# Rounding theta's number of turns by the integer result of one multiplication

## The chip, the cores and the metric

The kernel runs on one core of a Trainium2 chip. It is measured in device microseconds of one execution. A profiled execution also leaves a trace, in which each instruction has its engine, its start and its duration, and in which releases between engines can be followed. The engines are called as the profile calls them where rows are meant (PE, DVE, ACT, POOL, SP) and by name in the text: TensorE, VectorE, ScalarE, GpSimd, and SyncE, which issues the transfers.

## The reference, cut to what matters

An attention over 4 batches, 12 heads, 448 tokens with mixing across heads is followed by a gated block, and that by a block which turns every feature by an angle. The change lies in this last block:

```python
def _moe2_ref(x, w_theta, w_tok_r, w_tok_i, w_ch):
    theta = x @ w_theta                              # (4, 448, 768) @ (768, 768)
    cos_t, sin_t = (np.cos(theta), np.sin(theta))
    zr = x * cos_t
    zi = x * sin_t
    yr = np.einsum('ts,bsd->btd', w_tok_r, zr)
    yi = np.einsum('ts,bsd->btd', w_tok_i, zi)
    u = x + (yr + yi)
    return (u + np.maximum(u @ w_ch, 0.0)).astype(np.float32)
```

Theta reaches several turns, and the sine of ScalarE is fed with angles between -pi and pi, so the kernel takes whole turns off theta first.

## The kernel before

The program is written engine by engine in a fixed order: a list of units, each with functions to run before and after it (`d.unit`, `d.pre`, `d.post`), is walked once, and every engine executes its own instructions in the order in which they were written. Nothing reorders them later.

The last block, `moe2`, is the part of the program from about 614 us on. The tokens of a batch come in chunks of 128; batches are taken in pairs, so that the last 64 tokens of two batches make one common chunk (c = 3): 14 chunks of two halves of 384 features, 28 halves in all. The units stand in this order: theta for the four chunks of batch 0 and the first chunk of batch 1; `tok` for batch 0 (six units, the product with w_tok); theta for the other two chunks of batch 1; `ch` for batch 0 (six units, the product with w_ch); `tok` for batch 1; theta for batch 2, and so on to `ch` for batch 3.

A theta unit is 18 matmuls (six slices of the contraction, three products of high and low parts of x and w_theta, L555). After the first half come six transposes of x into PSUM (L1053). PSUM has eight buffers of this kind, and TensorE waits when the next isn't released.

- `angles` (L1059 to L1073), one call for each half, runs behind the half's theta unit. On VectorE: n = theta / 2pi plus a large constant (L1064), the constant off again (L1065), which leaves the nearest whole number; r = theta - n C1 (L1067) and r - n C2 (L1068), where C1 + C2 = 2pi; then r is held between -pi and pi (L1069). On ScalarE: the absolute value of r, its sine as cosine, and the sine of r (L1070 to L1072). L1064 and L1067 read theta from PSUM; the others read SBUF.
- `rotate` (L1075 to L1094) is called one unit later, so VectorE has the angles of a half ahead of the rotation of the half before. VectorE multiplies x (in PSUM) by cosine and sine (L1091, or four half-height instructions L1087 for the common chunk), ScalarE rounds the products to the high part (`d.cast`, L548), and GpSimd takes the rest as the low part of z (`d.rest`, L551).
- `split_x2` (L1023) does the same for x itself, two chunks ahead: two casts on ScalarE, and two operations "x2s" on GpSimd (L551), for every second half. The theta of that chunk needs them.
- For the chunk of batch 1 among the first five, `rotate` is put off until the six `tok` units, so its PSUM buffers stay taken until then. Beside these `tok` units VectorE also adds the residual (L1114), splits u (L551) and turns four blocks of w_ch from 64-bit into two 32-bit numbers (L983 to L996, L988 with an operand of type uint32).

In a steady row of theta units VectorE repeats, for every half: L1091 twice (the half before), L1064, L1065, L1067, L1068, L1069. This is called a turn below. Between two turns of a chunk GpSimd runs two operations of z, and in every second turn the two of x2 as well.

Of the kernel before, what the change touches and what calls it, by code (L numbers as in the profile page):

```python
# [9 lines left out]
I32 = mybir.dt.int32  # L10
U32 = mybir.dt.uint32
AF = mybir.ActivationFunctionType
ALU = mybir.AluOpType
# [467 lines left out]
TO = ((1, 1, 1, 1, 1, 1), (1, 0, 1, 0, 1, 0), (1, 0, 1, 0, 1, 1), (0, 1, 1, 1, 1, 0))  # L481
KC = 4
KE = 3
MAGIC = 12582912.0
INV2PI = 1.0 / (2.0 * math.pi)
C1 = 6.28125
C2 = 2.0 * math.pi - C1
# [454 lines left out]
def moe2(d, left, win_es, last_u, m1_left):  # L942
    tc, nc, io = d.tc, d.nc, d.io
# [115 lines left out]
    def angles(b, c, half):  # L1059

        th = st.pop((b, c, half))
        tp = d.pools["t2"]
        n = tp.tile([128, 384], F32, tag="n", name="n")
        nc.vector.tensor_scalar(out=n, in0=th, scalar1=INV2PI, scalar2=MAGIC, op0=ALU.mult, op1=ALU.add)  # L1064
        nc.vector.tensor_scalar(out=n, in0=n, scalar1=MAGIC, scalar2=None, op0=ALU.subtract)  # L1065
        r = tp.tile([128, 384], F32, tag="r", name="r")
        nc.vector.scalar_tensor_tensor(out=r, in0=n, scalar=-C1, in1=th, op0=ALU.mult, op1=ALU.add)  # L1067
        nc.vector.scalar_tensor_tensor(out=r, in0=n, scalar=-C2, in1=r, op0=ALU.mult, op1=ALU.add)  # L1068
        nc.vector.tensor_scalar(out=r, in0=r, scalar1=PI_F, scalar2=-PI_F, op0=ALU.min, op1=ALU.max)  # L1069
        nc.scalar.activation(out=n, in_=r, func=AF.Abs)  # L1070
        nc.scalar.activation(out=n, in_=n, func=AF.Sin, scale=-1.0, bias=d.const["hpi"])
        nc.scalar.activation(out=r, in_=r, func=AF.Sin)  # L1072
        st[b, c, half] = ((n, r), st[b, c, "x"][half])  # L1073
# [119 lines left out]
    for b, c, i0 in chunks:  # L1193
        for half in range(2):
            d.post(i0 + half, angles, b, c, half)
# [104 lines left out]
```

## Time and profile before

| | us |
|---|---|
| three runs | 913.23, 915.72, 919.0 |
| median | 915.72 |
| profiled execution | 918.77 |
| its span, first to last instruction | 917.0 |
| VectorE busy in it | 679.8 |
| TensorE busy in it | 857.6 |

The span is 1.8 us shorter than the profiled execution's own time, which also holds what lies around the program. Starts in the rows are counted from the span's start. The granted clock is a share of TensorE's full speed: 1.00 is 2.4 GHz, 0.50 is 1.2 GHz. A row "x2" merges two instructions of one kind that follow each other. A bracket behind a row is the idle time of the engine just before it and what ended it; matmul ends are modelled, and spans on GpSimd are rough.

### The profile page before, as it was taken

To read this page: it belongs to the slowest core of one execution; us is meant where nothing else is said; L and a number is where in the kernel's file an instruction comes from. 1 tells how busy PE (TensorE), PEld (TensorE's weight loads), DVE (VectorE), ACT (ScalarE), POOL (GpSimd) and SP (SyncE) were. 2 spreads that over 40 slices of the span, in tenths; PEclk is the share of its full clock that TensorE was granted. 3 is DMA by queue.
4 is the path that set the end of the run, shared out by engine and by line. 5 is a ranking of instruction groups with operands and counts; after the bars stand their busy time and mean duration, and the time that the engine had idled before them with its cause. 6 is when DMAs were issued, how large, how long until landed. Compare 5 with 4: busy or idle time off the path is not lost.

```text
span 917.0 us, 29432 instructions
## 1 busy us (share of the span) xinstructions
PE 857.6 (94%) x12008; PEld 675.2 (74%) x12008; DVE 679.8 (74%) x1509; ACT 525.3 (57%) x1188; POOL 252.1 (27%) x453
## 2 busy tenths in 40 slices
PE   8789899999989999697899999999998999999998
PEld 2345556555656566486797988889897999999997
DVE  3787888788878887389989899859878349539421
ACT  5688789878988896365554655425535025315110
POOL 0163255225322632000000000015606316604511
PEclk9999999999999999899999999989998999999999
DMA  6557656765676545773376685896620302210301
GB/s 205 179 192 224 197 179 219 223 204 179 218 222 214 174 158 138 260 233 108 119 246 213 190 256 172 267 339 213 231 89 19 121 18 53 71 50 18 93 29 61
DMA packets 116343, 151.15 MB, mean 165 GB/s; under 512 B 26224, under 2 KB 100208, under 8 KB 116208
## 3 DMA queue, kind: packets, MB, share of 16 engines
q1 hardware_dynamic: 116208, 149.26, 51.3%
q8 instruction: 95, 1.56, 0.7%
q14 instruction: 40, 0.33, 0.1%
HBM read 78.38 MB, written 32.31 MB: 121 GB/s over the span
## 4 chain that ended last, share of the span: by engine, by line
PE 54%; DVE 22%; DMA 9%; ACT 5%; issue 5%; POOL 3%; SPq 1%; ACTq 0%; DVEq 0%; POOLq 0%
PE ps L555 30%; PE psC L302 7%; PE psB L244 6%; PE psA L219 5%; PE psD L354 5%; DMA blk<-s 2%; DVE da L611 2%; ACT e L258 2%; POOL vl L197 1%; DMA win<-win_d 1%; DVE dp L605 1%; ACT s L225 1%; DMA x2T<-xres 1%; DVE da L592 1%; DMA xraw<-xT 1%
## 5 line engine op out<-in xcount | busy, mean ns | idle before, releaser
L258 ACT ACTIVATE e<-psB,nmx 128x448 f32<-128x448 f32 x180 | 112.7, 634 | 33.8 <-DVE nmx L250 32.0
L331 DVE SCALAR_TENSOR_TENSOR al<-psC,ah 128x480 f16<-128x480 f32 x180 | 116.3, 647 | 16.0 <-ACT ah L325 15.1
L250 DVE TENSOR_REDUCE nmx<-psB 128x1 f32<-128x448 f32 x180 | 103.9, 618 | 18.8 <-PE psB L244 17.2
L302 PE MATMUL psC<-wr,e 64*64 64x60 f32 x5632 | 106.9, 221 | 10.9 <-issue 8.9
L302 PEld LDWEIGHTS psC<-wr,e 64*64 64x64 f32 x5632 | 93.5, 135 | 23.4 <-issue 11.5
L551 POOL TENSOR_TENSOR x2s<-x,x2s 128x384 fp32r<-128x384 f32 x28 | 29.6, 1082 | 288.1 <-DMA wth<-wth_d 213.4
L555 PE MATMUL ps<-wtok,z 128*128 128x448 f32 x504 | 104.8, 368 | 0.4 <-POOL z L551 0.4
L219 PE MATMUL psA<-k,q 64*64 64x448 f32 (+2 forms) x768 | 95.2, 549 | 9.1 <-ACT s L225 5.5
L244 PE MATMUL psB<-blk,kpre 64*64 64x448 f32 x720 | 102.0, 548 | 1.6 <-DMA blk<-s 0.8
L325 ACT ACTIVATE ah<-psC 128x480 f16<-128x480 f32 x180 | 93.2, 576 | 16.5 <-PE psC L302 16.2
L555 PEld LDWEIGHTS ps<-wtok,z 128*128 128x128 f32 x504 | 94.4, 188 | 10.0 <-POOL z L551 0.8
L354 PEld LDWEIGHTS <-vh 128*64 128x64 f16 x1536 | 56.6, 111 | 57.2 <-issue 52.8
L555 PE MATMUL ps<-wth,x2s 128*128 128x384 f32 x504 | 94.3, 343 | 2.1 <-DVE r L1067 1.1
L555 PEld LDWEIGHTS ps<-wth,x2s 128*128 128x128 f32 x504 | 89.3, 192 | 3.0 <-DVE r L1067 1.5
L225 ACT ACTIVATE s<-psA 124x896 f32<-124x896 f32 (+1 forms) x90 | 83.7, 930 | 13.0 <-PE psA L219 5.4
L555 PE MATMUL ps<-u,wch 128*128 128x448 f32 x432 | 89.9, 368 | 0.0
L555 PEld LDWEIGHTS ps<-u,wch 128*128 128x128 f32 x432 | 81.1, 188 | 8.1
L551 POOL TENSOR_TENSOR z<-zz,z 128x384 fp32r<-128x384 f32 x56 | 61.9, 1126 | 71.4 <-ACT z L548 71.3
L555 PE MATMUL ps<-win,x 128*128 128x512 f32 x252 | 63.3, 405 | 10.7 <-DVE x L551 6.4
L264 POOL TENSOR_SCALAR rc<-sum 128x2 f32<-128x2 f32 (+1 forms) x92 | 22.5, 244 | 179.1 <-ACT e L258 178.0
L280 POOL TENSOR_SCALAR wr<-w,rc 128x60 f32<-128x60 f32 x180 | 54.2, 315 | 57.7 <-DVE rc L269 39.4
L244 PEld LDWEIGHTS psB<-blk,kpre 64*64 64x64 f32 x720 | 36.7, 133 | 44.0 <-issue 24.2
(129 smaller groups left out, 1577.5 us busy)
## 6 DMA issues: line engine op xcount, KB each, us to landing
blk<-s SPq DMA_DIRECT2D x176, 210.0 KB
draw<-in_w_in SPq DMA_DIRECT2D x24, 256.0 KB
k<-in_kvT SPq DMA_DIRECT2D x24, 224.0 KB
xraw<-xT SPq DMA_DIRECT2D x24, 224.0 KB
xres<-xT SPq DMA_DIRECT2D x24, 224.0 KB
x2T<-xres SPq DMA_DIRECT2D x24, 224.0 KB
xres<-x2T SPq DMA_DIRECT2D x24, 224.0 KB
out<-uu SPq DMA_DIRECT2D x24, 224.0 KB
```

Of the source, the lines that this page charges most:

```text
L219: nc.tensor.matmul(ps[e][r, :S], q[p, o + r.start:o + r.stop], k[p], start=True, stop=True)
L225: nc.scalar.activation(out=out, in_=pair[:m, :, :S], func=AF.Copy, scale=0.125)
L244: nc.tensor.matmul(ps[e][c:c + 64, :S], kpre[k, e], blk[k], start=True, stop=True)
L250: nc.vector.tensor_reduce(out=nmx[r][:, e:e + 1], in_=ps[:, :S], axis=AX.X, op=ALU.max, negate=True)
L258: nc.scalar.activation(out=x, in_=ps[:, :S], func=AF.Exp, bias=m[:, e:e + 1], accum_out=sm[:, e:e + 1])
L280: nc.gpsimd.tensor_scalar(out=w, in0=wts[n], scalar1=rc[:, e:e + 1], scalar2=0.0, op0=ALU.mult, op1=ALU.add)
L302: nc.tensor.matmul(pc[r][h][c:c + 64, jc, :, SQ * e:SQ * e + SQ], x[p, c:c + 64], wr[r][e][p], start=(e == 0 and jc == 0), stop=(e == 1 an ...
L325: nc.scalar.activation(out=at_view(r, e, at[b, t][0]), in_=at_src(r, e), func=AF.Copy, scale=2.0 ** -17)
L331: nc.vector.scalar_tensor_tensor(out=al, in0=at_src(r, e), scalar=2.0 ** -17, in1=ah, op0=ALU.mult, op1=ALU.subtract)
L354: nc.tensor.matmul(ps[p, o:o + n], v[:, jc, p], a[:, i0:i0 + n], start=(o == 0 and m == 0), stop=(o > TI and m == len(terms) - 1))
L551: eng.tensor_tensor(out=out, in0=in_, in1=hi.bitcast(F32), op=ALU.subtract)
L555: self.nc.tensor.matmul(ps, l, r, start=(i == 0), stop=(i == len(terms) - 1))
```

## The change

One multiplication now writes its result as int32 into the same buffer, and the engine's conversion does the rounding. The two multiply-adds read these integers as their first operand. The constant and the instruction that took it off again are gone. The buffer is later overwritten with fp32 by ScalarE, as before. Every half has one VectorE instruction less; no other engine's instructions change or move, and no transfer does.

```diff
-MAGIC = 12582912.0
...
         n = tp.tile([128, 384], F32, tag="n", name="n")
-        nc.vector.tensor_scalar(out=n, in0=th, scalar1=INV2PI, scalar2=MAGIC, op0=ALU.mult, op1=ALU.add)
-        nc.vector.tensor_scalar(out=n, in0=n, scalar1=MAGIC, scalar2=None, op0=ALU.subtract)
+        turns = n.bitcast(I32)
+        nc.vector.tensor_scalar(out=turns, in0=th, scalar1=INV2PI, scalar2=None, op0=ALU.mult)
         r = tp.tile([128, 384], F32, tag="r", name="r")
-        nc.vector.scalar_tensor_tensor(out=r, in0=n, scalar=-C1, in1=th, op0=ALU.mult, op1=ALU.add)
-        nc.vector.scalar_tensor_tensor(out=r, in0=n, scalar=-C2, in1=r, op0=ALU.mult, op1=ALU.add)
+        nc.vector.scalar_tensor_tensor(out=r, in0=turns, scalar=-C1, in1=th, op0=ALU.mult, op1=ALU.add)
+        nc.vector.scalar_tensor_tensor(out=r, in0=turns, scalar=-C2, in1=r, op0=ALU.mult, op1=ALU.add)
         nc.vector.tensor_scalar(out=r, in0=r, scalar1=PI_F, scalar2=-PI_F, op0=ALU.min, op1=ALU.max)
```

Here L1064 stays the multiplication, and the three instructions that are L1067, L1068 and L1069 before are L1066, L1067 and L1068 after.

## Rows read from the trace of the kernel before

**Rows 1.** The page, part 1: busy us (share of span) xinstructions.

```profile
PE 857.6 (94%) x12008; PEld 675.2 (74%) x12008; DVE 679.8 (74%) x1509; ACT 525.3 (57%) x1188; POOL 252.1 (27%) x453
```

**Rows 2.** TensorE's waits from 600 us on: us in total, times, longest.

```profile
PE ps L1053 <- issue: 2.6, 1, 2.6
PE ps L555 <- DVE r L1067: 1.1, 1, 1.1
PE ps L555 <- POOL x2s L551: 1.0, 1, 1.0
PE ps L555 <- POOL z L551: 0.4, 1, 0.4
```

**Rows 3.** TensorE in order of time from 600 us: start, us, what, [idle before].

```profile
624.40 0.82 PE L1053 MATMUL ps<-ident,x 128*128 128x128 f32 x6
...
638.83 3.74 PE L555 MATMUL ps<-wth,x2s 128*128 128x384 f32 x20
...
686.77 0.49 PE L1053 MATMUL ps<-ident,x 128*128 128x128 f32 x3
689.91 0.87 PE L1053 MATMUL ps<-ident,x 128*128 128x128 f32 x3 [2.65 <-issue]
691.89 5.49 PE L555 MATMUL ps<-wth,x2s 128*128 128x384 f32 x18 [1.11 <-DVE r L1067]
697.22 22.48 PE L555 MATMUL ps<-u,wch 128*128 128x448 f32 x108
...
769.48 0.81 PE L1053 MATMUL ps<-ident,x 128*128 128x128 f32 x6
...
773.28 22.48 PE L555 MATMUL ps<-u,wch 128*128 128x448 f32 x108
```

**Rows 4.** Busy times and granted clock (PEclk) in one stretch.

```profile
691.90:697.20 5.30, 5.30 (x18) 5.30 (x19) 5.13 (x9) 3.21 (x7) 2.38 (x3) 0.57 0.26 74
```

**Rows 5.** VectorE and GpSimd in order of time, single turns of the theta loop.

```profile
623.76 0.36 DVE L1069 TENSOR_SCALAR r<-r 128x384 f32<-128x384 f32 x1
623.86 2.12 POOL L551 TENSOR_TENSOR x2s<-x,x2s 128x384 fp32r<-128x384 f32 x2 [13.07 <-ACT x2s L548]
...
630.19 0.36 DVE L1065 TENSOR_SCALAR n<-n 128x384 f32<-128x384 f32 x1
...
630.88 2.30 POOL L551 TENSOR_TENSOR z<-zz,z 128x384 fp32r<-128x384 f32 x2 [2.34 <-ACT z L548]
...
631.17 1.13 DVE L1068 SCALAR_TENSOR_TENSOR r<-n,r 128x384 f32<-128x384 f32 x1
...
632.34 1.06 DVE L1069 TENSOR_SCALAR r<-r 128x384 f32<-128x384 f32 x1
...
634.83 0.65 DVE L1065 TENSOR_SCALAR n<-n 128x384 f32<-128x384 f32 x1
...
635.52 2.30 POOL L551 TENSOR_TENSOR z<-zz,z 128x384 fp32r<-128x384 f32 x2 [0.25 <-ACT z L548]
636.10 0.85 DVE L1068 SCALAR_TENSOR_TENSOR r<-n,r 128x384 f32<-128x384 f32 x1
636.98 1.05 DVE L1069 TENSOR_SCALAR r<-r 128x384 f32<-128x384 f32 x1
```

**Rows 6.** VectorE in order of time, halves outside those turns.

```profile
624.97 0.55 DVE L1064 TENSOR_SCALAR n<-ps 128x384 f32<-128x384 f32 x1
...
654.79 0.48 DVE L1065 TENSOR_SCALAR n<-n 128x384 f32<-128x384 f32 x1
...
690.30 0.94 DVE L1065 TENSOR_SCALAR n<-n 128x384 f32<-128x384 f32 x1
691.28 0.55 DVE L1067 SCALAR_TENSOR_TENSOR r<-n,ps 128x384 f32<-128x384 f32 x1
```

**Rows 7.** Two lines of VectorE: ns min/median/max, first and last start, forms.

```profile
L1068 DVE SCALAR_TENSOR_TENSOR r<-n,r x28: 557/862/1141, 620.7 to 848.5; 128x384 f32<-128x384 f32 x28
...
L988 DVE TENSOR_TENSOR ch<-ch,wchraw x4: 558/559/561, 664.1 to 685.5; 128x384 f32<-128x384 f32 x4
```

## The prediction

> **What bounds the kernel now.** I read the page's busy times first, then TensorE's waits, then TensorE's work in order of time, and last the single instructions around the edited lines. The busy times say that TensorE works 94% of the span and VectorE 74% [rows 1], so a shorter VectorE program is worth only what TensorE loses by waiting for it. The edited lines run from 619 us on, once for each half of a 128-token chunk, 28 times. From 600 us to the end TensorE stands idle only four times [rows 2]: 1.0 us for the low part of x2 that GpSimd makes, 0.4 us for a z from GpSimd, 2.65 us before three transposes, and 1.11 us for L1067 [rows 2, 3]. The order of time shows where they lie: the first after 642.57 us (638.83 + 3.74), the last two between 686.77 and 697.22 us [rows 3]. After 697 us TensorE never waits again, so nothing that VectorE gains there reaches the end.
>
> What the last two waits cost is more than their length. From the transposes at 686.77 to the next matmuls by w_ch at 697.22 are 10.45 us; the same six transposes and eighteen matmuls of batch 2 take 3.80 us, from 769.48 to 773.28 [rows 3]. The loss is 6.65 us: 2.65 + 1.11 of waiting, and 2.89 us because the matmuls behind the wait run at a low clock. The eighteen take 5.49 us [rows 3], and in their stretch the granted clock is 0.57, which is 1.2 GHz for most of it and 2.4 GHz after [rows 4]; the low clock follows the two waits. So all that this change can win is 1.0 + 0.4 + 6.65 = 8.1 us.
>
> **The change, part by part.** *The instruction taken out (L1065).* It takes 0.36 us alone and 0.65 us where a GpSimd operation runs beside it, and 0.03 to 0.04 us lie between two instructions (L1068 ends at 632.30, L1069 starts at 632.34) [rows 5]. Twenty-eight times 0.36 are 10.1 us of VectorE, but what counts is how much earlier VectorE reaches three points: 640 us (first wait), 689.9 us (the buffer of the transposes) and 691.8 us (end of L1067).
>
> *A turn of the loop.* Between 625 and 652 us VectorE repeats a turn for each half: two multiplications for z, L1064, L1065, L1067, L1068, L1069. Two L1069 in a row start at 632.34 and 636.98, 4.64 us apart [rows 5], though L1065 takes 0.36 in the one turn and 0.65 in the next. Its longer time was paid for by L1068, which takes 1.13 us in the first and 0.85 in the second, against 0.56 at best [rows 5, 7]. So the turn is not the sum of VectorE's instructions. GpSimd's pair of z operations runs from 630.88 to 633.18; L1069, 0.36 us alone, is issued at 632.34 and ends at 633.40, 0.22 behind the pair [rows 5]. The pair itself starts only after ScalarE's work on the L1069 before it. Two engines take turns at something: the one that started first finishes, the other stands. A row shows that it goes the other way too: at 623.76 L1069 starts 0.10 us ahead of a GpSimd pair and takes its bare 0.36 us [rows 5].
>
> Without L1065, L1068 starts earlier by 0.36 + 0.03 us in the plain turn, at 630.78 instead of 631.17, and by 0.65 + 0.03 in the other, at 635.42 instead of 636.10. GpSimd's z pairs start at 630.88 and 635.52. So L1068 now comes 0.10 us before GpSimd instead of 0.29 or 0.58 behind, the same lead as at 623.76. I take it to win.
>
> *The turn then.* Plain turn: L1068 runs 0.56 us, to 631.34. GpSimd's first z operation ends 0.88 us behind it (in the trace the pair ends at 633.18, 0.88 after L1068's end at 632.30), at 632.22; L1069 ends 0.22 behind that, at 632.44 instead of 633.40: 0.96 us less. In the other kind of turn GpSimd has two x2 operations between; the second z operation ends 0.88 after L1069, the x2 pair about 2.0 us later (2.12 at 623.86, with a short wait in it [rows 5]), L1068 waits for it and ends about 0.4 behind (an estimate: 0.56 less what it does before it stands), the next z operation 0.88 behind that and L1069 0.22 more: about 4.4 us instead of 4.64, 0.25 less. Six turns, three of each kind: 3 x (0.96 + 0.25) = 3.6 us.
>
> The Trainium skill (SBUF — State Buffer, "SBUF: two separate sides") says that a VectorE operation in a two-port mode, or with two SBUF inputs against a GpSimd operation that reads SBUF, and a GpSimd operation hold the shared port pair alone, for the whole instruction, by who starts first. The rows above agree (0.36 us against 1.06 for L1069). A sum of bare durations would give 0.39 in each turn, 2.3 us in six, and would leave about 1 us of waiting below (some 7 us won in all); by this rule the outcome hangs on 0.1 us, 3.6 us in six turns if VectorE is first and nothing if GpSimd is.
>
> *The rest up to 690 us.* The first two halves save up to 0.39 each, but the third theta leaves TensorE only just ahead of the transposes at 624.40 [rows 3], and its L1064 starts at 624.97 [rows 6]: 0.5 in all. The half at 654.79 saves 0.48 + 0.03 [rows 6], the one after it 0.36 + 0.03. Together 0.5 + 3.6 + 0.5 + 0.4 = 5.0 us at 689.9, and another 0.94 + 0.03 at L1067, because the L1065 before it took 0.94 us [rows 6].
>
> *What TensorE then meets.* First wait: by 640 us VectorE is 0.5 + 0.25 + 0.96 + 0.25 = about 2.0 us ahead, more than the 1.0. The second (0.4) goes with it. TensorE reaches the place of the third wait, 686.77 + 0.49 = 687.26 in the trace, at 687.26 - 1.4 = 685.86; the buffer comes at 689.91 - 5.0 = 684.9. It needs L1067 some 0.3 us later, behind three transposes, at 686.2, and has it at 691.28 + 0.55 - 5.0 - 0.97 = 685.9 [rows 3, 6]. All four waits close, the last with 0.3 us to spare, and with them the low clock.
>
> *The multiplication with an integer result (L1064), and L1067 and L1068 that read it.* No row shows fp32 to int32, or an int32 operand beside an fp32 one. The nearest: L988 multiplies fp32 by a uint32 operand and takes 0.558 us, as L1068 does with two fp32 operands (0.557) [rows 7]. Below: a gain on L1064 isn't excluded, but it still reads as much and writes as much in one pass, so I put it at a tenth of its 0.55 us at most [rows 6], 28 x 0.05 = 1.5 us of VectorE, hidden once the waits are closed. Above: twice the present length, 0.55 us more for each of the three. I take no cost, since L988 is the nearest row.
>
> **Sum.** 8.1 us off the profiled execution, 918.77 - 8.1 = 910.7 us. The median of the three runs is 915.72, 3.05 us below that execution: 915.72 - 8.1 = 907.6 us.
>
> **Rivals.** *A, GpSimd still first (18%).* If L1068 comes 0.1 us later than I work out, it waits for the first z operation as now, the pair still ends when it did, and turns stay 4.64 us. Then VectorE gains 0.5 + 0.5 + 0.4 = 1.4 us up to 689.9 and 0.97 more at L1067, and the low clock stays: 2.4 us, 913.3. For it: the lead of 0.10 us is small. Against it: 623.76, where the same lead was enough.
>
> *B, the clock falls all the same (8%).* If a shorter wait is left between 685 and 692 us and the granted clock still halves, 2.9 us of the 8.1 stay: 5.2 us, 910.5. For it: the last margin is 0.3 us. Against: the clock is whole in all the later stretches without a wait.
>
> *C, integers are dear (4%), the other side.* If L1064, L1067 and L1068 each take twice as long, L1068 asks at 631.17 - 0.39 + 1.09 = 631.87, as GpSimd's first operation ends, and itself takes 0.56 more between the two: turns of 5.2 us. Six turns lose 3.4 us, the four halves outside them 1.2 each, the L1065 at 690.30 gives back some: about 9 us at L1067, all of it TensorE's wait: 925. It decides from about 0.1 us more per instruction (then A) and becomes a loss from about 0.4 on. Against it stands L988. The Trainium skill (VectorE: DVE Perf Modes, "Specifications") says the engine computes in fp32 and converts integer operands, with no price for it; L988's 0.558 us agrees.
>
> That the change does not do what it says I give nothing: the program built from it has 28 VectorE instructions fewer, and every engine's order is otherwise the same.
>
> **Chances.** Forecast 70%, A 18%, B 8%, C 4%. About 1% is what a measurement of this kernel tells from no change (the runs shown lie between 913.23 and 919.0); 1% is 9.2 us, a little more than all that there is to win. The forecast's 8.1 us may show as more than that in a third of its cases or somewhat more: faster 0.26. Half of C is slower by over 1%; with a little for what I have not seen, 0.03. The rest, 0.71, is within 1%. The range takes in the forecast less 3 us of spread, and A plus 1.2: 904.5 to 914.5.
>
> **What will show it.** L1064 at 0.54 us and the two readers at 0.55 and 0.56. In the loop L1068 before GpSimd's z at 0.56 us, GpSimd's first z operation at about 1.5 us, and L1069 to L1069 alternately 3.7 and 4.4 us. No wait of TensorE after 620 us, a granted clock of 1.00 from 685 to 700 us, and all of TensorE's work after 697 us the same but 8 us earlier. It is wrong if the turns stay at 4.64 us, if L1064 is longer by 0.1 us, or if TensorE meets a new wait behind the ones that closed, such as GpSimd's z or x2 now late by VectorE's being first.

## The result, and the profile after

The changed kernel takes 907.83 us, the median of ten runs (903.05 to 913.75); the kernel before, run beside it, takes 915.82 us (913.23 to 920.99, ten runs). The ratio is 0.9907, with an interval of 0.9887 to 0.9927. The forecast was 907.6 us.

The profiled execution of the changed kernel took 913.75 us, the longest of its ten, with a span of 912.0, only 5.0 less than before, so the gain must be looked for inside the stretch that the change touches. The first rows are TensorE's waits from 600 us on (us in total, times, longest), the answer to [rows 2]:

```profile
PE ps L554 <- DVE g L550: 0.9, 1, 0.9
PE ps L554 <- DVE r L1066: 0.5, 1, 0.5
```

The wait for g lies ahead of the last block. Of the four waits in [rows 2] a remnant of 0.5 us is left. TensorE in order of time in the same kernel (start, us, what, idle before), beside [rows 3]:

```profile
616.79 3.29 PE L554 MATMUL ps<-wth,x2s 128*128 128x384 f32 x18
...
641.25 6.52 PE L554 MATMUL ps<-wth,x2s 128*128 128x384 f32 x36
...
687.50 1.02 PE L1052 MATMUL ps<-ident,x 128*128 128x128 f32 x6
689.00 3.39 PE L554 MATMUL ps<-wth,x2s 128*128 128x384 f32 x18 [0.49 <-DVE r L1066]
692.24 22.48 PE L554 MATMUL ps<-u,wch 128*128 128x448 f32 x108
```

Before, the first theta matmul stands here:

```profile
614.35 3.31 PE L555 MATMUL ps<-wth,x2s 128*128 128x384 f32 x18
```

From the first theta matmul to the first one by w_ch it was 697.22 - 614.35 = 82.87 us [rows 3]; now it is 692.24 - 616.79 = 75.45, which is 7.42 us less. This is called the stretch below. Behind it nothing differs: from there to the end of the span are 219.8 us in both. Ahead of it the two programs are the same, and this one execution came 2.44 us later to the theta block than the other; that is why the profiled spans differ by 5.0 and not 7.4. The six transposes and eighteen matmuls ahead of w_ch now take 4.74 us (687.50 to 692.24), beside 10.45 before and 3.80 in batch 2. The eighteen take 3.39 us where they took 5.49, and the granted clock around them is whole (start and end, length, busy times, then PEclk), beside 0.57 in [rows 4]:

```profile
680.00:700.00 20.00, 19.50 (x109) 18.29 (x108) 18.26 (x32) 9.96 (x21) 9.06 (x8) 1.00 0.14 39
```

The turns are the answer to [rows 5]: VectorE and GpSimd of the changed kernel in order of time. L1067 is now the second multiply-add, L1068 the clamp.

```profile
629.46 1.06 DVE L1068 TENSOR_SCALAR r<-r 128x384 f32<-128x384 f32 x1
...
632.53 0.56 DVE L1067 SCALAR_TENSOR_TENSOR r<-n,r 128x384 f32<-128x384 int32 x1
632.62 2.43 POOL L550 TENSOR_TENSOR z<-zz,z 128x384 fp32r<-128x384 f32 x2 [1.24 <-ACT z L547]
...
633.12 1.05 DVE L1068 TENSOR_SCALAR r<-r 128x384 f32<-128x384 f32 x1
...
635.00 2.00 POOL L550 TENSOR_TENSOR x2s<-x,x2s 128x384 fp32r<-128x384 f32 x2
...
636.20 1.22 DVE L1067 SCALAR_TENSOR_TENSOR r<-n,r 128x384 f32<-128x384 int32 x1
...
637.45 1.05 DVE L1068 TENSOR_SCALAR r<-r 128x384 f32<-128x384 f32 x1
```

The second multiply-add starts at 632.53, 0.09 us ahead of GpSimd's z, and takes its bare 0.56 us. From clamp to clamp are 3.66 us (629.46 to 633.12), and 4.33 where a pair of x2 lies between (633.12 to 637.45); both were 4.64. The three lines with integers (ns min/median/max, first and last start, forms), beside [rows 6, 7]:

```profile
L1064 DVE TENSOR_SCALAR n<-ps x28: 540/542/560, 621.3 to 838.7; 128x384 int32<-128x384 f32 x28
L1066 DVE SCALAR_TENSOR_TENSOR r<-n,ps x28: 553/555/556, 621.9 to 839.2; 128x384 f32<-128x384 int32 x28
L1067 DVE SCALAR_TENSOR_TENSOR r<-n,r x28: 557/559/1249, 622.5 to 839.8; 128x384 f32<-128x384 int32 x28
```

VectorE is busy for 664.1 us, 15.7 less than in [rows 1], though the 28 instructions taken out are worth 10.1 at their bare length; the other 5.6 us was standing that counted as busy (the second multiply-add alone went from 25.4 to 19.6 us in all).

### The profile page after: what moved, and what is told of

The parts are those of the page before. It is cut to its first block, busy times and chain, and to the rows that moved or that the text cites. A ratio compares the mean times of both kernels' runs of the same rounds, so it can differ in the third digit from the quotient of the medians.

```text
span 912.0 us, 29404 instructions
## 1 busy us (share of the span) xinstructions
PE 856.9 (94%) x12008; PEld 673.8 (74%) x12008; DVE 664.1 (73%) x1481; ACT 526.1 (58%) x1188; POOL 254.4 (28%) x453
## 4 chain that ended last, share of the span: by engine, by line
PE 66%; DVE 15%; DMA 7%; issue 4%; ACT 4%; POOL 3%; SPq 1%; ACTq 0%; DVEq 0%; POOLq 0%
PE ps L554 39%; PE psC L302 8%; PE psB L244 6%; PE psA L219 6%; PE psD L354 5%; DMA blk<-s 3%; DVE da L610 2%; DMA win<-win_d 2%; ACT s L225 1%; POOL vl L197 1%; DVE dp L604 1%; DVE da L591 1%; ACT e L258 1%; DVE da L590 1%; DVE dp L596 1%
## 5 line engine op out<-in xcount | busy, mean ns | idle before, releaser
L302 PE MATMUL psC<-wr,e 64*64 64x60 f32 x5632 | 105.9, 221 | 12.3 <-issue 10.3
L554 PE MATMUL ps<-wth,x2s 128*128 128x384 f32 x504 | 91.9, 337 | 0.5 <-DVE r L1066 0.5
L554 PEld LDWEIGHTS ps<-wth,x2s 128*128 128x128 f32 x504 | 87.2, 188 | 0.9 <-DVE r L1066 0.7
L550 POOL TENSOR_TENSOR z<-zz,z 128x384 fp32r<-128x384 f32 x56 | 64.8, 1175 | 56.6 <-ACT z L547 56.5
L547 ACT ACTIVATE u<-xres 128x448 fp32r<-128x448 f32 x24 | 13.9, 577 | 99.1 <-DVE xres L1113 99.1
```

Of the source, the lines that this page charges most:

```text
L302: nc.tensor.matmul(pc[r][h][c:c + 64, jc, :, SQ * e:SQ * e + SQ], x[p, c:c + 64], wr[r][e][p], start=(e == 0 and jc == 0), stop=(e == 1 an ...
L550: eng.tensor_tensor(out=out, in0=in_, in1=hi.bitcast(F32), op=ALU.subtract)
L554: self.nc.tensor.matmul(ps, l, r, start=(i == 0), stop=(i == len(terms) - 1))
```

## The experiments

Ratios are to the kernel before, run beside it on the same chip. All but the one without GpSimd's z start from the changed kernel. The waits and the stretch (from the first theta matmul to the first one by w_ch, 82.87 us in the kernel before) are those of one profiled execution each.

| experiment | us, median (runs) | ratio, interval | waits of TensorE after 610 us | stretch, us |
|---|---|---|---|---|
| changed kernel | 907.83 (10) | 0.9907, 0.9887 to 0.9927 | 0.5 | 75.45 |
| 1 column copied ahead | 907.93 (6) | 0.9919, 0.9896 to 0.9943 | 0.5 | 75.38 |
| 1 column copied behind | 907.06 (6) | 0.9907, 0.9884 to 0.9930 | 0.5 | 75.47 |
| 48 columns ahead | 905.89 (7) | 0.9905, 0.9871 to 0.9940 | 0.5 | 75.46 |
| 192 columns ahead | 912.96 (12) | 0.9957, 0.9936 to 0.9978 | 2.3, 1.0, 0.6, 0.4 | 79.57 |
| 192 columns behind | 908.22 (9) | 0.9911, 0.9878 to 0.9944 | 0.5 | 75.57 |
| integers, and back | 916.07 (10) | 1.0018, 0.9994 to 1.0041 | 2.6, 1.4, 1.1, 0.4 | 83.21 |
| before, without GpSimd's z | 905.76 (4) | 0.9890, 0.9864 to 0.9915 | none | 74.70 |
| buffers held longer | 915.33 (10) | 0.9986, 0.9955 to 1.0017 | 4.6 | 82.44 |
| NO2 = 2 | 909.15 (9) | 0.9930, 0.9900 to 0.9959 | 0.5, 0.4 | 75.85 |
| NO2 = 1 | 915.73 (12) | 0.9996, 0.9974 to 1.0018 | 0.8, 0.8, 0.6, 0.6, 0.5, 0.5 | 79.85 |

### Integers, and back to floating point

The integers alone, without the shorter list: the removed instruction's place is taken by a conversion.

```diff
         nc.vector.tensor_scalar(out=turns, in0=th, scalar1=INV2PI, scalar2=None, op0=ALU.mult)
+        nc.vector.tensor_copy(n, turns)
...
-        nc.vector.scalar_tensor_tensor(out=r, in0=turns, scalar=-C1, in1=th, op0=ALU.mult, op1=ALU.add)
+        nc.vector.scalar_tensor_tensor(out=r, in0=n, scalar=-C1, in1=th, op0=ALU.mult, op1=ALU.add)
```

(The second multiply-add likewise.)

> The changed kernel with the integers turned back to fp32 by one more VectorE instruction (128x384, SBUF to SBUF) in the place of the instruction that was taken out; both multiply-adds read fp32 as before. It does the conversion alone and keeps the count of instructions. Theory: the integer result by itself gives and costs nothing: the new instruction takes 0.36 us alone, turns 4.64 us, the four waits as before, 915.7 us, ratio 1.000 (0.998 to 1.002). Rival (the integer result itself makes the gain, or costs something that the shorter list hides): below 911 or above 919 us.

Measured: 916.07 us, ratio 1.0018. TensorE in order of time, then the conversion's line:

```profile
690.28 0.87 PE L1052 MATMUL ps<-ident,x 128*128 128x128 f32 x3 [2.64 <-issue]
692.26 5.43 PE L554 MATMUL ps<-wth,x2s 128*128 128x384 f32 x18 [1.11 <-DVE r L1067]
...
L1065 DVE CAST n<-n x28: 359/361/943, 620.1 to 847.8; 128x384 f32<-128x384 int32 x28
```

The waits of 2.64 and 1.11 us and the eighteen slow matmuls are back, to a few hundredths [rows 3]. Writing integers neither wins nor costs, to within the interval of 0.9994 to 1.0041 (that reading them costs nothing is seen from the 555 and 559 ns above); all of the gain hangs on the instruction that is gone.

### Something put back: one column

```diff
         nc.vector.tensor_scalar(out=turns, in0=th, scalar1=INV2PI, scalar2=None, op0=ALU.mult)
+        nc.vector.tensor_copy(d.const["sin"], st[b, c, "x"][half][:, :1])
```

> The changed kernel with one small VectorE copy (128x1, from PSUM, about 0.16 us and 0.03 us to the next start) between the multiplication L1064 and the multiply-add L1067 of every half. Theory (who starts first keeps the other standing): the second multiply-add loses its lead of 0.10 us over GpSimd's z and waits for it again; turns of the loop go back to 4.64 us although VectorE is still 0.2 us shorter per half than before; TensorE's waits of 1.0, 0.4 and about 3 us and the half clock behind them come back; about 914.4 us, ratio to before 0.998. Rival (bare durations add up): each half gives back 0.19 of 0.39 us, turns of about 4.4 us in the mean, half of the gain stays, about 911.5 us.

The control has the same copy behind the second multiply-add:

> The changed kernel with the same small VectorE copy, but between the second multiply-add and the clamp of every half. Theory: it lies where VectorE waits for GpSimd anyway, so turns stay 3.67 and 4.33 us; only the halves outside the loop pay 0.19 us each; 908.0 to 908.8 us, ratio 0.992. Rival (bare durations): the same loss as with the copy ahead, about 911.5 us.

Measured: ratios 0.9919 and 0.9907. The first missed its expectation, and VectorE's rows say why:

```profile
628.35 0.54 DVE L1064 TENSOR_SCALAR n<-ps 128x384 int32<-128x384 f32 x1
628.81 0.14 DVE L1065 COPY sin<-ps 128x1 f32<-128x1 f32 x1
628.92 0.55 DVE L1067 SCALAR_TENSOR_TENSOR r<-n,ps 128x384 f32<-128x384 int32 x1
```

The copy takes 0.14 us and starts while the multiplication still runs. From L1064 to the first multiply-add are 0.57 us, as without it (628.27 - 627.70 in the changed kernel). Nothing was delayed, so these two runs tell nothing of the order. The control's 907.06 us lies below the 908.0 to 908.8 expected, for the same reason: its copy cost nothing either.

### Something put back: 192 and 48 columns

```diff
+        idle = tp.tile([128, 192], F32, tag="idle", name="idle", bufs=1)
+        nc.vector.tensor_copy(idle[:, :192], st[b, c, "x"][half][:, :192])
```

Ahead of the two multiply-adds:

> The changed kernel with a VectorE copy of 192 columns from PSUM between the multiplication and the first multiply-add. The one-column copy of the run before took 0.145 us but moved nothing behind it (0.58 us from the multiplication to the first multiply-add, as without it), so that run could not decide; 191 columns more should push the multiply-adds back by about 0.2 us, and the second one from 0.10 us ahead of GpSimd's z to 0.10 us behind. Theory: it then stands until GpSimd's first operation ends, turns go back to 4.64 us, TensorE's waits near 643, 655 and 687 to 692 us come back with the half clock; 913 to 915 us, ratio 0.997 to 0.999. Rival (bare durations): 0.2 of 0.39 us is given back per half; turns about 4.2 us in the mean, about 909 to 911 us.

Behind them, so that VectorE's list is as long and only the place differs:

> The changed kernel with the same copy of 192 columns behind the second multiply-add, before the clamp. Theory: the second multiply-add keeps its lead, the copy lies in the time in which the clamp stands for GpSimd; turns stay 3.67 and 4.33 us, 907 to 908.5 us, ratio 0.991 to 0.992. Rival (bare durations): as with the copy ahead.

Ahead, but with 48 columns:

> The changed kernel with a copy of 48 columns between the multiplication and the first multiply-add: about 0.05 us, half of the lead of 0.10 us. Theory: the second multiply-add still starts first, turns stay 3.7 and 4.35 us, 908 us, ratio 0.992; with the run of 192 columns this shows a switch between 0.05 and 0.2 us and no slope. Rival (a slope, 0.05 us for each half): 0.5 us, which no comparison of times can tell, but turns would be longer by 0.05 in each kind and no switch would show at 192 columns.

With 192 columns ahead, VectorE and GpSimd in order of time:

```profile
626.89 0.54 DVE L1064 TENSOR_SCALAR n<-ps 128x384 int32<-128x384 f32 x1
627.35 0.34 DVE L1066 COPY idle<-ps 128x192 f32<-128x192 f32 x1
627.62 0.54 DVE L1068 SCALAR_TENSOR_TENSOR r<-n,ps 128x384 f32<-128x384 int32 x1
...
628.16 2.30 POOL L550 TENSOR_TENSOR z<-zz,z 128x384 fp32r<-128x384 f32 x2 [1.25 <-ACT z L547]
628.19 1.40 DVE L1069 SCALAR_TENSOR_TENSOR r<-n,r 128x384 f32<-128x384 int32 x1
...
632.83 1.38 DVE L1069 SCALAR_TENSOR_TENSOR r<-n,r 128x384 f32<-128x384 int32 x1
```

The copy delays the first multiply-add by 0.73 - 0.57 = 0.16 us. The second one then starts 0.03 us behind GpSimd's z instead of 0.09 ahead, takes 1.40 us instead of 0.56, and the turn is 4.64 us again (628.19 to 632.83). Six delays of 0.16 us make 1 us; TensorE's waits add up to 4.3 us (5.2 before). The same copy behind the multiply-adds leaves only the wait of 0.5 us; the second multiply-add (L1067) keeps its lead of 0.10 us, and from clamp to clamp (L1070) are 3.67 us:

```profile
631.02 0.90 DVE L1070 TENSOR_SCALAR r<-r 128x384 f32<-128x384 f32 x1
...
633.95 0.56 DVE L1067 SCALAR_TENSOR_TENSOR r<-n,r 128x384 f32<-128x384 int32 x1
...
634.05 2.42 POOL L550 TENSOR_TENSOR z<-zz,z 128x384 fp32r<-128x384 f32 x2 [1.24 <-ACT z L547]
...
634.69 0.90 DVE L1070 TENSOR_SCALAR r<-r 128x384 f32<-128x384 f32 x1
```

Between the two places lie 0.9957 - 0.9911 = 0.46%, 4.2 us, by the ratios, whose intervals overlap a little, and 79.57 - 75.57 = 4.00 us by the stretch. Both lists are equally long, so the place ahead of GpSimd is what counts.

The runs with 48 columns moved nothing either: the multiply-add starts 0.57 us behind L1064, and the copy is hidden as the single column was. They do not narrow down where the switch lies.

I had expected 913 to 915 us with the copy ahead; 912.96 us came, and half of the gain stayed. The rival's turns of about 4.2 us did not come. In the profiled execution the waits are back, but the clock did not fall behind them (it is 1.00 from 685 to 700 us). Whether it stays whole in the other executions is not shown.

```profile
686.79 0.52 PE L1052 MATMUL ps<-ident,x 128*128 128x128 f32 x3 [2.28 <-issue]
687.94 3.39 PE L554 MATMUL ps<-wth,x2s 128*128 128x384 f32 x18 [0.62 <-DVE r L1068]
```

### The kernel before, without GpSimd's z

If the turn is GpSimd's holding of VectorE, then taking GpSimd away must shorten it with VectorE's program as it was.

```diff
             d.cast(h[:, fs], zz)
-            d.rest(nc.gpsimd, l[:, fs], zz, h[:, fs])
+            d.cast(l[:, fs], zz)
```

> The kernel before, with its four-instruction rounding, but the low part of z is written by a ScalarE cast instead of GpSimd's subtraction (so the low part of z is left out of the result). Theory: without GpSimd's z the clamp and the second multiply-add take 0.36 and 0.56 us, the turn is VectorE's own sum of about 3.5 us or ScalarE's of about 3.6 us, the waits of TensorE after 620 us close although nothing was taken off VectorE's list; about 908 us, ratio 0.991. Rival (the turn of 4.64 us is VectorE's own work): turns stay near 4.6 us and the time near 915.7 us.

Measured: 905.76 us, ratio 0.9890, as large a gain as that of the change, without one instruction off VectorE's list. TensorE in order of time, and VectorE's clamp (which is L1069 here):

```profile
680.52 0.82 PE L1053 MATMUL ps<-ident,x 128*128 128x128 f32 x6
681.28 3.39 PE L555 MATMUL ps<-wth,x2s 128*128 128x384 f32 x18
...
L1069 DVE TENSOR_SCALAR r<-r x28: 359/360/1197, 617.6 to 834.2; 128x384 f32<-128x384 f32 x28
```

No wait is left between them, and the clamp's median falls to its bare 0.36 us; in the changed kernel it is 1.05. Turns are 4.20 and 3.36 us (L1064 starts at 628.27, 632.47 and 635.83), and not 3.5 or 3.6 throughout: where the two of x2 still run on GpSimd, L1065 stands (1.19 us at 628.85). So the length of VectorE's own list did not set the turn. The run has one limit: it also frees GpSimd itself, for whose x2 and z the first two waits (1.4 us) were; the last two were for VectorE.

### Buffers held longer

Is the low clock a follower of the wait, or did it happen to stand there? Eight copies of 384 columns ahead of one `rotate` make the wait larger again, in the changed kernel.

```diff
         css, x = st.pop((b, c, half))
+        if (b, c, half) == (1, 0, 0):
+            hold = d.pools["t2"].tile([128, 384], F32, tag="zz0", name="hold")
+            for _ in range(8):
+                nc.vector.tensor_copy(hold, x)
```

> The changed kernel with eight copies of 384 columns from PSUM at one place, before the rotation of the chunk of batch 1 whose PSUM buffers TensorE waits for at 688 us: VectorE is held up once by about 4 us there and nowhere else. It brings back the third and fourth wait alone. Theory (the low clock follows the wait): TensorE waits about 4 us longer, the granted clock halves behind it, and the 18 matmuls of theta take about 5.4 us instead of 3.39; 907.9 + 4.2 + 2 to 3 us = 914 to 915 us. Rival (the low clock was chance, not the wait's): only the wait, 912 us, and 3.39 us for the 18 matmuls.

Measured: 915.33 us, ratio 0.9986. TensorE in order of time, then a stretch with its granted clock:

```profile
686.87 0.87 PE L1052 MATMUL ps<-ident,x 128*128 128x128 f32 x3 [4.56 <-issue]
687.88 5.82 PE L554 MATMUL ps<-wth,x2s 128*128 128x384 f32 x18
...
686.40:693.20 6.80, 6.19 (x20) 5.82 (x21) 6.59 (x12) 4.19 (x9) 3.87 (x4) 0.50 0.20 58
```

Behind a wait of 4.56 us the clock is 0.50, which is 1.2 GHz, for 6.80 us, and the eighteen matmuls take 5.82 us instead of 3.39. The stretch is 82.44 - 75.45 = 7.0 us longer than in the changed kernel; the ratios differ by 0.79%, 7.2 us. Here wait and clock together make the price, as the prediction counted it; with 192 columns ahead the waits alone did.

### More cover for the gates' g

One wait is left ahead of the last block. NO2 is the number of out units of batch 2 that stand before the gates of batch 3; with fewer, more of them come behind.

```diff
-NO2 = 3
+NO2 = 2
```

> The changed kernel with NO2 = 2 instead of 3: of the six output units of batch 2 in the gated block one more stands behind the gates of batch 3 (12 matmuls, about 2.5 us), where TensorE waits 2.08 and 0.92 us for VectorE's rest of g and the granted clock halves behind it (611 to 618 in the changed kernel's record of the clock, some 597 to 604 of the span). Theory (what a wait costs is the wait and the half clock behind it; cover closes both): the two waits fall below 0.7 us together, the clock stays whole, 3 to 5 us less than the changed kernel, 903 to 905 us, ratio to before 0.986 to 0.988. Rival (the wait moves: VectorE is the bound there and g comes later by as much as the cover is long, or a wait opens before the gates): within 1 us of the changed kernel.

> As the run before with NO2 = 1: two more output units, about 5 us of cover. Theory: nothing more than with NO2 = 2 where that closes the waits, since only 3.0 us of wait is there to be covered; the same time within 1 us, or slower if the gates now wait for the normalized v, whose VectorE work has one unit less in front. Rival: as above.

Measured: ratios 0.9930 and 0.9996; the theory's 0.986 to 0.988 did not come. With 2 nothing was gained (the interval overlaps that of the changed kernel), and with 1 the gain of the change was lost to new waits: four for x2s in the theta units (0.6, 0.5, 0.8 and 0.8 us) and, ahead of the gates, one of 2.03 us for ScalarE's vn. With 2, ScalarE, VectorE and TensorE in order of time:

```profile
588.11 0.58 ACT L547 ACTIVATE g<-gt 128x448 fp32r<-128x448 f32 x1 [8.35 <-PE ps L554]
588.72 0.62 DVE L550 TENSOR_TENSOR g<-gt,g 128x448 fp32r<-128x448 f32 x1 [4.23 <-ACT g L547]
...
593.19 0.88 PE L554 MATMUL ps<-g,wout 128*128 128x448 f32 x3 [2.08 <-DVE g L550]
```

TensorE's 2.08 us for VectorE's g stay to the hundredth, because ScalarE's cast of g waits 8.35 us for TensorE: batch 2's out units still read the buffers of g. In both kernels that cast starts 3.00 us ahead of the end of those matmuls. So the work meant as cover is itself what the wait is for, and the wait moves with it; this is read from the rows, and no edit tested it.

## Why the prediction was right, and where it was off

**What could be won: right.** It said 8.1 us, of four waits and one stretch at half clock. In the stretch itself 7.42 us came, and the ratio of the medians says 8.5 (6.7 to 10.3 by its interval). The parts were off both ways: up to the transposes 1.71 us came (686.77 - 614.35 against 687.50 - 616.79) where 1.0 + 0.4 were counted, and from there to w_ch 10.45 - 4.74 = 5.71 instead of 6.65. That the median came within 0.2 us of the forecast 907.6 is luck: the interval alone is 1.8 us to either side, and the stretch gave 0.7 us less than was forecast. Nothing came from outside: the work behind w_ch kept its length.

**The turns: right, by the reason given.** The forecast of 3.7 and about 4.4 us met 3.66 and 4.33, and the lead of 0.10 us met 0.09. That it is the order of the two engines, and not the bare lengths, is shown from two sides: with GpSimd's z away the old list gains as much, and 0.16 us ahead of the multiply-adds undo the turn while the same work behind them does not. Rival A, with its 18%, was thus 0.1 to 0.2 us away; it is a true alternative, not a remote one. The Trainium skill (SBUF — State Buffer, "SBUF: two separate sides") says that whoever starts first on the shared ports holds them for the whole instruction; the traces agree (0.56 us when VectorE starts 0.09 ahead, 1.40 when it starts 0.03 behind).

**VectorE's lead up to 690 us: 4.35 us, not 5.0.** Counted from the first theta matmul, L1064 of the half concerned starts as follows (starts of the rows less 614.35 or 616.79):

| half | before | after | ahead by | forecast |
|---|---|---|---|---|
| third | 10.62 | 10.91 | -0.29 | 0.5 |
| ninth | 39.85 | 35.66 | 4.19 | 4.1 |
| tenth | 50.35 | 46.39 | 3.96 | 4.6 |
| eleventh | 75.37 | 71.02 | 4.35 | 5.0 |

The rows of the ninth to eleventh half before, and of the third and the same three after:

```profile
654.20 0.56 DVE L1064 TENSOR_SCALAR n<-ps 128x384 f32<-128x384 f32 x1
...
664.70 0.56 DVE L1064 TENSOR_SCALAR n<-ps 128x384 f32<-128x384 f32 x1
...
689.72 0.55 DVE L1064 TENSOR_SCALAR n<-ps 128x384 f32<-128x384 f32 x1
```

```profile
625.61 2.10 POOL L550 TENSOR_TENSOR x2s<-x,x2s 128x384 fp32r<-128x384 f32 x2 [12.42 <-ACT x2s L547]
625.67 1.17 DVE L1068 TENSOR_SCALAR r<-r 128x384 f32<-128x384 f32 x1
...
627.70 0.54 DVE L1064 TENSOR_SCALAR n<-ps 128x384 int32<-128x384 f32 x1
...
652.45 0.56 DVE L1064 TENSOR_SCALAR n<-ps 128x384 int32<-128x384 f32 x1
...
652.98 2.30 POOL L550 TENSOR_TENSOR z<-zz,z 128x384 fp32r<-128x384 f32 x2
...
654.44 1.05 DVE L1068 TENSOR_SCALAR r<-r 128x384 f32<-128x384 f32 x1
...
663.18 0.56 DVE L1064 TENSOR_SCALAR n<-ps 128x384 int32<-128x384 f32 x1
...
687.81 0.55 DVE L1064 TENSOR_SCALAR n<-ps 128x384 int32<-128x384 f32 x1
```

The terms outside the turns were taken as bare lengths, against the prediction's own reasoning. At the second half the clamp had been 0.10 us ahead of GpSimd's x2 [rows 5]; after the change GpSimd starts 0.06 us ahead, at 625.61, and the clamp takes 1.17 us instead of 0.36. So the 0.5 forecast there became a loss of 0.29. The same happened to the ninth half's clamp (1.05 us at 654.44 instead of 0.36), where 0.5 had been forecast and 0.23 was lost. The turns made good most of it: 4.48 us in six instead of 3.6, since four, not three, were of the short kind.

**All four waits close: nearly.** Three did. At L1066 the lead missed 0.65 us, and TensorE came 0.3 us earlier than counted (1.71 instead of 1.4); together that is 0.96 us against a spare of 0.3, so 0.49 us of wait and 0.20 in the transposes (1.02 us beside 0.82) are left.

**The clock stays whole: right,** although not by closing the wait entirely. Rival B was half met: a shorter wait did remain, and the clock did not fall behind it. In the kernel before, the clock had fallen with the wait of 2.65 us, before that of 1.11 began: it was 0.95 from 687.20 to 689.90 us and 0.50 from there to 691.90.

**Integers cost nothing: right.** 542, 555 and 559 ns, and the run with the conversion back, whose interval around 1 is 0.9994 to 1.0041. Rival C falls.

## What to carry to other kernels

When two engines hold each other up, an instruction is not worth its duration but what it does to the order in which they start: here 0.16 us per turn, put in the wrong place, cost about 4 us, and the same work a step later nothing. Follow such an order through every half, the first and the last ones too, because the engine that loses in one place may win in another. And before moving work in as cover for a wait, look whether that very work still reads the buffers that the wait is for.

## What the runs showed of the hardware

- An independent VectorE copy of 1 or 48 columns (0.14 and 0.19 us) between the multiplication and the multiply-add that reads its result delayed the latter by nothing (0.57 us from start to start with and without it); one of 192 columns (0.34 us) delayed it by 0.16 us.
- How the clock answers a wait is not settled by the wait's length: behind 2.65 us (before) and 4.56 us (buffers held) TensorE ran at 1.2 GHz for about 6.8 us, behind 2.28 and then 0.62 us (192 columns ahead) it stayed at 2.4 GHz. Nor is it settled by the program: ahead of the last block TensorE waits 2.08 us and then about 1 us in the changed kernel (0.92) and with one column copied ahead (1.04), with the same code there. The first row is the changed kernel's, the other two are those of the copied column: low for 6.80 us in the one, for some 3.3 in the other. What decides between these was not tried.

```profile
599.90:606.70 6.80, 5.88 (x17) 4.78 (x16) 5.51 (x14) 1.54 (x4) 0.00 (x0) 0.50 1.10 350
...
595.90:599.20 3.30, 3.30 (x10) 2.55 (x9) 3.11 (x9) 0.61 (x2) 0.00 (x0) 0.50 1.09 351
599.20:602.70 3.50, 3.50 (x18) 3.24 (x18) 1.94 (x6) 0.00 (x0) 0.00 (x0) 0.99 1.08 387
```
